# Blocks 4 and 5 of two weights loaded and converted one by one, three identity products fewer, and another order of the opening

## The chip, the core and the metric

The kernel runs on one core of a Trainium2 chip. Its engines run side by side, each through its own list of instructions in order: TensorE (PE in the profile, with its weight loads as PEld), VectorE (DVE), ScalarE (ACT), GpSimd (POOL), and SyncE (SP), which here only issues DMAs. They wait for each other through semaphores. The metric is device time in microseconds of one execution; lower is better. A time is the median of several runs.

## What is computed

Eight batches of eight heads, 576 tokens of 64 numbers each, first go through an attention over 32 memories, then all 4608 tokens through a bilinear feed-forward layer. Cut to what matters:

```python
def _attn_ref(q, k, v, phi):
    a = phi - np.max(phi, axis=2, keepdims=True)
    a = np.exp(a)
    a = a / (np.sum(a, axis=2, keepdims=True) + 1e-09)
    k_m = np.einsum('bhsm,bhsd->bhmd', a, k)
    v_m = np.einsum('bhsm,bhsd->bhmd', a, v)
    scores = scale * np.matmul(q, k_m.transpose(0, 1, 3, 2))
    scores = scores - np.max(scores, axis=-1, keepdims=True)
    attn = np.exp(scores)
    attn = attn / (np.sum(attn, axis=-1, keepdims=True) + 1e-09)
    return np.matmul(attn, v_m)

def _moe_ref(x, w1, w2, w3, w_out):       # 512 -> 1024 -> 1024 -> 512
    return ((x @ w1) * (x @ w2) @ w3) @ w_out
```

The four weights arrive as float64.

## The kernel before

**Weights first.** w3 and w_out have no function between them, so the kernel multiplies them once, in the opening: W = w3 w_out, by blocks of 128 rows k = 0 to 7 of the inner index. w3 is taken transposed and in two halves, w30 and w31; w30 gives the upper half of W (tokens X0 to X2 and W01 to W07 of the order, four PSUM banks), w31 the lower half (W10 to W17). `product` (lines 493 to 505) makes one such step: with all four row blocks it is four matmuls of 512 columns in float32, eight passes in the trace. X0, X1 and X2 are step 0 of w30 in pieces.

**Conversion.** No engine computes in float64, so each block is loaded as raw words (`raw`) and converted in five steps, C1 to C5 (`convert`, lines 422 to 489): sign (VectorE; ScalarE for the last ones), high and low (ScalarE, which read the raw words), shift and join (VectorE). The joined block is `w` (of w3) or `wo` (of w_out). A task is one such block, or a pair of blocks; w1 and w2 are converted in the same way, by quarters of columns. `groups` (lines 380 to 385) lists the tasks by the raw buffer that they share; there are five raw buffers of one megabyte. When the three steps that read the raw words of a group are recorded, the load of the group five further on is issued from SP (`fetch`). Loads use eight semaphores in turn.

**Attention and the gated product.** Of batch 0, in the opening: top, exp, norm (maxima, exponentials and sums of phi), bm and bs (maxima spread on TensorE and taken off on VectorE), be (the exponentials by token), mem (the memories), memc (kvm, on ScalarE), block and blockc, sc, mx, sb, ex, sm, mu, tr (scores and softmax), ah and al (the probabilities as two float32r parts). M0 to M3 join the memories with w1 and w2, of which Mh and Ml make two parts. The gated product (`ab_unit`, tokens A, a, g) is 12 matmuls of 288 columns on TensorE (A), a copy `a_sb` on ScalarE (a) and a product into `g` on VectorE (g). The output follows from g with the weights W in two parts, Wh and Wl. K copies the upper half of W out of PSUM; Kh and r cast parts of it to Wh on ScalarE.

**What sets the order.** All engines keep the order in which the program records them, and for the first batch that order is the table FIRST, a list of tokens such as C1 (the next task's sign step), W01 or -exp. SECOND and BATCH do the same for the later batches. Identity products at the very start (WARM of them, line 581) keep TensorE busy until the first real product.

Of the kernel before, what the change touches and what calls it, by code (L numbers as in the profile page):

```python
# [24 lines left out]
FIRST = """
C1 C1 C3 C2 C2 C4 C3 C4 C5 C1 C3 C5 C1 C2 C4 C2 C3 C4 C5 C5 C1 C2 C3 C4 C1 C5 C2 C3 C3 C1 C4 C5 C2 C2 C2 C4 C4 C1 C5
C1 C3 C2 C3 C5 C1 C3 C4 C4 C5 C1 C2 C3 C4 C5 C5 C2 C4 C1 C3 C5 phi0 kv0 C1 C1 C2 C3 C2 q0 X0 X1 X2 W01 C3 C4 C4 C5 C5
W02 W03 W04 W05 W06 C2 C1 C1 C4 C2 C4 W07 C3 C2 C3 -top C5 K1 -exp C5 -bm -bs W10 Kh1 K3 C4 -norm C1 K0 -be C3 -mem C5
Kl1 Kt0 r0 Kt3 Kt1 -memc Kh3 -block r3 C2 C3 K2 s0 Kt2 Kh0 r1 s1 -blockc C4 C1 C5 W11 -sc0 -sc1 -scc0 -scc1 -mx1 -mx0
-sb0 -sb1 C3 C2 C4 -ex0 C2 C3 C1 C5 C1 -sm0 C4 C2 C4 C5 C3 C2 -mu0 -tr0 C4 C1 -ex1 C5 -sm1 C1 C2 C3 C5 -mu1 -tr1 C1  # L30
-ah0 -al0 W12 W13 W14 W15 W16 M0 Mh0 M1 C3 -ah1 Mh1 C2 W17 C4 Ml0 Ml1 Dt0 C4 A a -al1 g phi A A C2 a C3 a Et0 Dt3 g C5
g s3 f0 C1 C5 A A t0 Kh2 Kl2 a a g Et3 C2 M2 Mh2 Dt2 Dt1 g Ml2 A a A C1 C4 g f1 F3 F2 F0 a top g C3 r2 q A a A C1 a C5
g g C3 C4 C5 kv F1 f2 z0 A A D2 a a Kl0 D3 w2 y2 M3 Mh3 g g E2 Et2 Ml3 w3 A A h0 a a Kl3 y3 f3 s2 E3 bm g g bs w1 y1
h2 A a A D0 t2 g l2 Et1 E0 S2 z2 be mem A exp norm D1 E1 memc a a l0 g g block O blockc w0 y0 h1 l1 h4 h3 t3 l4 t1 z1
z3 M0 sc0 scc0 mx0 sb0 O O l3 O O Mh0 h6 S3 S1 l6 h5 Ml0 l5 O S4 h7 p4 p1 h11 ex0 l7 O O h9 h8 C11 sm0 mu0 tr0 l8 sc1
q M1 l9 O u2 ah0 h10 l10 O h12 p5 Mh1 h13 scc1 l11 al0 l12 l13 O O O O C21 C22 Ml1 mx1 sb1 ex1 C12 sm1
"""
# [12 lines left out]


# [770 lines left out]
```

## Time and profile before

| | |
|---|---|
| median of 3 runs | 521.74 us (520.87 to 522.21) |
| span of the profiled execution | 519.8 us |
| TensorE busy | 511.9 us, 98% |
| VectorE busy | 383.8 us, 74% |
| ScalarE busy | 280.1 us, 54% |
| GpSimd busy | 145.0 us, 28% |
| DMA | 68.86 MB, 132 GB/s over the span |

The page gives one profiled execution; its own time is known by its span, from its first to its last instruction. A share of busy time is a mean over the whole span. The first 100 us hold the opening and the first batch, in which ScalarE and VectorE are much busier than later; for these the trace is read by stretches. In a row of the timeline the brackets give the idle time before an instruction and what ended it.

### The profile page before, as it was taken

To read this page: it belongs to the slowest core of one execution; us is meant where nothing else is said; L and a number is where in the kernel's file an instruction comes from. 1 tells how busy PE (TensorE), PEld (TensorE's weight loads), DVE (VectorE), ACT (ScalarE), POOL (GpSimd) and SP (SyncE) were. 2 spreads that over 40 slices of the span, in tenths; PEclk is the share of its full clock that TensorE was granted. 3 is DMA by queue.
4 is the path that set the end of the run, shared out by engine and by line. 5 is a ranking of instruction groups with operands and counts; after the bars stand their busy time and mean duration, and the time that the engine had idled before them with its cause. 6 is when DMAs were issued, how large, how long until landed. Compare 5 with 4: busy or idle time off the path is not lost.

```text
span 519.8 us, 11002 instructions
## 1 busy us (share of the span) xinstructions
PE 511.9 (98%) x4488; PEld 443.5 (85%) x4488; DVE 383.8 (74%) x655; ACT 280.1 (54%) x494; POOL 145.0 (28%) x158
## 2 busy tenths in 40 slices
...
GB/s 282 413 407 352 386 149 131 228 1 129 167 163 2 115 221 121 3 25 188 245 3 0 153 297 8 2 115 236 107 1 28 216 215 1 1 69 24 2 1 91
DMA packets 29794, 68.86 MB, mean 132 GB/s; under 512 B 1840, under 2 KB 10032, under 8 KB 29744
## 3 DMA queue, kind: packets, MB, share of 16 engines
...
q14 instruction: 15, 0.12, 0.1%
...
## 4 chain that ended last, share of the span: by engine, by line
PE 91%; DMA 6%; issue 1%; ACT 1%; DVE 1%; SPq 0%; DVEq 0%; ACTq 0%
PE ab L596 39%; PE o L658 15%; PE x L658 14%; PE ab L658 6%; PE ab L346 3%; PE x L498 3%; PE x L224 3%; PE o L498 2%; DMA raw<-in_w_out 2%; DMA ph<-in_phiT 2%; PE ab L274 2%; PE o L346 1%; PE x L346 1%; DMA raw<-in_w3T 1%; PE x L233 1%
## 5 line engine op out<-in xcount | busy, mean ns | idle before, releaser
L596 PE MATMUL ab<-ah,mh 128*128 128x288 f32 x512 | 154.5, 302 | 0.0
L596 PE MATMUL ab<-ah,ml 128*128 128x288 f32 x512 | 151.6, 296 | 0.0
L596 PE MATMUL ab<-al,mh 128*128 128x288 f32 x512 | 149.4, 292 | 0.0
L641 DVE TENSOR_TENSOR sl<-g,sh 128x576 fp32r<-128x576 f32 x112 | 92.9, 848 | 24.8 <-ACT sh L635 24.6
L596 PEld LDWEIGHTS ab<-ah,mh 128*128 128x128 f32 x512 | 96.2, 188 | 9.2 <-DVE ss L305 4.2
L608 DVE TENSOR_TENSOR g<-ab,a_sb 128x288 f32<-128x288 f32 x128 | 57.8, 452 | 58.2 <-PE ab L596 36.2
L605 ACT COPY a_sb<-ab 128x288 f32<-128x288 f32 x128 | 51.2, 401 | 90.4 <-PE ab L596 89.1
L635 ACT CAST sh<-g 128x576 fp32r<-128x576 f32 x112 | 74.6, 677 | 45.9 <-PE o L658 20.2
L596 PEld LDWEIGHTS ab<-al,mh 128*128 128x128 f32 x512 | 97.4, 190 | 0.2 <-issue 0.2
L596 PEld LDWEIGHTS ab<-ah,ml 128*128 128x128 f32 x512 | 96.0, 188 | 0.0
L614 POOL TENSOR_TENSOR g<-g,g 128x288 f32<-128x288 f32 x32 | 26.0, 838 | 221.5 <-DVE g L608 221.5
L658 PE MATMUL o<-sh,Wh 128*128 128x288 f32 x192 | 56.8, 296 | 0.0
L658 PE MATMUL o<-sh,Wl 128*128 128x288 f32 x192 | 56.6, 295 | 0.0
L658 PE MATMUL o<-sl,Wh 128*128 128x288 f32 x192 | 56.6, 295 | 0.0
L622 POOL TENSOR_TENSOR g<-g,g 128x288 f32<-128x288 f32 x32 | 28.4, 906 | 90.3 <-DVE sl L641 80.6
L658 PE MATMUL x<-sh,Wh 128*128 128x288 f32 x176 | 52.9, 300 | 0.0
L658 PE MATMUL x<-sh,Wl 128*128 128x288 f32 x176 | 51.9, 295 | 0.0
L658 PE MATMUL x<-sl,Wh 128*128 128x288 f32 x176 | 51.9, 295 | 0.0
L658 PEld LDWEIGHTS x<-sh,Wh 128*128 128x128 f32 x176 | 33.1, 188 | 7.4 <-PE ab L274 4.2
L658 PEld LDWEIGHTS o<-sh,Wh 128*128 128x128 f32 x192 | 36.1, 188 | 1.4 <-issue 0.9
L626 POOL TENSOR_TENSOR g<-g,g 128x288 f32<-128x288 f32 x32 | 36.2, 1159 | 0.0
L658 PEld LDWEIGHTS o<-sh,Wl 128*128 128x128 f32 x192 | 36.1, 188 | 0.0
...
## 6 DMA issues: line engine op xcount, KB each, us to landing
...
```

The lines of the kernel that those rows point to most:

```text
L224: nc.tensor.matmul(ps[t][h * M : (h + 1) * M, : 2 * D], lhsT=v["a"][:, (NT * i + t) * P + h * M : (NT * i + t) * P + (h + 1) * M], rhs=kvt ...
L346: nc.tensor.matmul(ps[t][g * M : (g + 1) * M], lhsT=vm[b % 2][d, g], rhs=w12_sb[q][d, :, g], start=True, stop=True,)
L498: nc.tensor.matmul(pw[r][i][:, cols], lhsT=x[:, i * P : (i + 1) * P], rhs=wos[k // half][:, k % half, cols], start=k == 0 and cols.start == 0,
L596: nc.tensor.matmul(banks[w][:, :HALF], lhsT=x[:, t, w, fc : fc + P], rhs=y[:, n, t * HALF : (t + 1) * HALF], start=i == 0, stop=i == len(t ...
L605: nc.scalar.copy(out=a_sb, in_=banks[0][:, :HALF])
L608: nc.vector.tensor_tensor(out=G[n, f // half][:, f % half], in0=banks[1][:, :HALF], in1=a_sb, op=ALU.mult)
L614: nc.gpsimd.tensor_tensor(out=low, in0=top, in1=low, op=ALU.subtract)
L622: gp(out=s2, in0=s2, in1=s3, op=ALU.subtract)
L626: gp(out=a12, in0=a12, in1=s2, op=ALU.subtract)
L635: nc.scalar.copy(out=hi, in_=src)
L641: nc.vector.tensor_tensor(out=lo, in0=src, in1=hi.bitcast(F32), op=ALU.subtract)
L658: nc.tensor.matmul(ps[j][:, :HALF], lhsT=piece(x, s, 2 * part + k)[:, jc], rhs=y[:, k], start=i in (1, 4, 2, 5) and part == 0 and k == 0 a ...
```

## The change

Blocks 4 and 5 of w30 and of w_out become single tasks, as blocks 0 to 3 are; before, each was a pair. Groups 4 and 5 then hold one block of both weights each, where they held the pair of w30 and the pair of w_out. The number of groups and of bytes stays. WARM goes from 18 to 15. FIRST is written in another order, with ten tokens more (two tasks more, of five steps each). SECOND and BATCH hold the same tokens as before, with other line breaks, and the lines behind FIRST have numbers higher by one.

```diff
-WARM = 18
+WARM = 15
 FIRST = """
-C1 C1 C3 C2 C2 C4 C3 C4 C5 C1 C3 C5 C1 C2 C4 C2 C3 C4 C5 C5 C1 C2 C3 C4 C1 C5 C2 C3 C3 C1 C4 C5 C2 C2 C2 C4 C4 C1 C5
...
+C1 C2 C2 C1 C3 C2 C4 C3 C2 C4 C5 C1 C5 X0 C3 C4 C3 C5 C1 C2 C4 C5 C1 C4 C3 X1 C2 C3 C5 C4 C1 C1 C2 C3 C5 C4 C2 C2 C1
...
-    groups += [[("w30", k, 1, slice(0, DF // 2)), ("wo", k, 1, slice(0, DF // 2))] for k in range(1, 4)]
-    groups += [[(kind, k, 2, slice(0, DF // 2))] for k in (4, 6) for kind in ("w30", "wo")]
+    groups += [[("w30", k, 1, slice(0, DF // 2)), ("wo", k, 1, slice(0, DF // 2))] for k in range(1, 6)]
+    groups += [[(kind, k, 2, slice(0, DF // 2))] for k in (6,) for kind in ("w30", "wo")]
```

Three places in the lists of the engines, a row for one instruction or a run of equal ones.

VectorE, the conversion of block 1 (L457 or L458 is a sign step, L482 or L483 a shift, L487 or L488 a join; `w_137` and `w_132` are blocks 0 and 1 of w30, `wo_84` is w_out's, `raw` of the second sign step without `w` is block 2's). Before:

```order
L457 TENSOR_SCALAR uw<-raw 128x512
L487 ISA w_137<-w_137,u 128x1024
L457 TENSOR_SCALAR u<-raw 128x512
L482 TENSOR_SCALAR wo_84<-wo_84 128x512
L487 ISA wo_84<-wo_84,uw 128x1024
```

And now:

```order
L488 ISA w_132<-w_132,u 128x1024
L483 TENSOR_SCALAR wo_84<-wo_84 128x512
L458 TENSOR_SCALAR uw<-raw 128x512
L458 TENSOR_SCALAR u<-raw 128x512
L488 ISA wo_84<-wo_84,uw 128x1024
```

The shift of w_out's block 1 moved ahead of the sign step of w30's block 2, its join stays behind it.

SP, the loads from block 3 on (`in_w3T` in the first rows is w30, later w31; `ph` and `a` are phi in its two layouts). Before:

```order
L419 DMA raw<-in_w3T 128x1024
L419 DMA raw<-in_w_out 128x1024
L419 DMA raw<-in_w3T 128x2x1024
L419 DMA raw<-in_w_out 128x2x1024
L419 DMA raw<-in_w3T 128x2x1024
L419 DMA raw<-in_w_out 128x2x1024
L419 DMA raw<-in_w3T 128x2x1024 x3
L144 DMA ph<-in_phiT 128x2x576
L146 DMA a<-in_phi_tok 128x1152
L154 DMA kv_223<-in_kv 128x2x1024
```

And now, from block 4 on:

```order
L420 DMA raw<-in_w3T 128x1024
L420 DMA raw<-in_w_out 128x1024
L420 DMA raw<-in_w3T 128x1024
L420 DMA raw<-in_w_out 128x1024
L420 DMA raw<-in_w3T 128x2x1024
L420 DMA raw<-in_w_out 128x2x1024
L420 DMA raw<-in_w3T 128x2x1024
L145 DMA ph<-in_phiT 128x2x576
L147 DMA a<-in_phi_tok 128x1152
L420 DMA raw<-in_w3T 128x2x1024
L155 DMA kv_225<-in_kv 128x2x1024
```

Block 4 of both weights comes ahead of block 5 of either; phi moved ahead of two pairs of w31, kv ahead of one. The last pair of w31 comes behind kv, ahead of q, in both.

ScalarE, the last instructions ahead of the conversion of w1's first quarter (`w_0_78`; L517 or L518 are the casts to Wh). Before:

```order
L517 CAST Wh_82<-raw_89 128x256
L517 CAST Wh_82<-raw_93 128x256
L472 ACTIVATE w_393<-raw 128x1024
L478 ACTIVATE uw<-raw 128x1024
L544 COPY raw_88<-ab 128x512
L517 CAST Wh_82<-raw_86 128x256
L517 CAST Wh_82<-raw_91 128x256
L478 ACTIVATE u<-raw 128x1024
L472 ACTIVATE w_0_78<-raw 128x1024
```

And now:

```order
L518 CAST Wh_82<-raw_89 128x256
L518 CAST Wh_82<-raw_91 128x256
L473 ACTIVATE w_390<-raw 128x1024
L246 ACTIVATE kvm<-ab,sm 128x128 x2
L479 ACTIVATE u<-raw 128x1024
L473 ACTIVATE w_400<-raw 128x1024
L518 CAST Wh_82<-raw_88 128x256
L479 ACTIVATE uw<-raw 128x1024
L545 COPY raw_86<-ab 128x512
L473 ACTIVATE w_0_78<-raw 128x1024
```

Two more such casts stood higher up in the list before, none does now: six came ahead of w1, now three, and the other three stand among the steps of the first batch's gated product.

## Rows read from the trace of the kernel before

**Rows 1.** The page, busy time, share of the span, instructions, by engine:

```profile
PE 511.9 (98%) x4488; PEld 443.5 (85%) x4488; DVE 383.8 (74%) x655; ACT 280.1 (54%) x494; POOL 145.0 (28%) x158
```

**Rows 2.** Stretches: length, then busy time of each engine, clock, DMA:

```profile
core 0: us, PE busy (x) PEld busy (x) DVE busy (x) ACT busy (x) POOL busy (x), PEclk, DMA share, GB/s
...
10.00:12.00 2.00, 1.92 (x5) 0.58 (x4) 1.18 (x4) 1.63 (x4) 0.00 (x0) 1.00 1.01 377
12.00:14.00 2.00, 0.43 (x1) 0.30 (x2) 1.86 (x5) 1.81 (x3) 0.00 (x0) 1.00 1.02 416
...
20.00:22.00 2.00, 1.88 (x5) 0.68 (x4) 1.94 (x3) 1.86 (x3) 0.00 (x0) 1.00 1.02 408
...
120.00:519.00 399.00, 396.45 (x3732) 366.90 (x3712) 284.99 (x486) 184.73 (x353) 107.80 (x114) 1.00 0.28 95
```

**Rows 3.** Timeline, TensorE's waits: start, length, engine, instruction, idle before:

```profile
13.56 6.71 PE L498 MATMUL ab<-wo,w 128*128 128x512 f32 x15 [1.65 <-DVE wo L487]
...
24.80 14.00 PE L498 MATMUL ab<-wo,w 128*128 128x512 f32 x32 [0.28 <-DVE wo L487]
...
41.26 1.95 PE L498 MATMUL x<-wo,w 128*128 128x512 f32 x4 [0.53 <-DVE a L212]
...
46.13 0.59 PE L254 MATMUL ab<-ident,kvm 128*128 128x128 f32 x2 [0.56 <-ACT kvm L245]
```

**Rows 4.** Stretches from 55 to 100 us, columns as in rows 2:

```profile
55.00:60.00 5.00, 5.00 (x13) 2.24 (x12) 4.90 (x9) 4.95 (x6) 0.00 (x0) 1.00 1.04 385
60.00:65.00 5.00, 5.00 (x13) 2.25 (x12) 4.96 (x7) 4.70 (x6) 0.00 (x0) 1.00 1.05 388
65.00:70.00 5.00, 5.00 (x33) 1.84 (x40) 4.12 (x8) 4.04 (x6) 0.00 (x0) 1.00 0.41 153
70.00:75.00 5.00, 5.00 (x30) 2.42 (x15) 4.14 (x9) 4.82 (x7) 0.00 (x0) 1.00 0.26 89
75.00:80.00 5.00, 5.00 (x40) 5.00 (x39) 4.29 (x8) 4.65 (x7) 0.23 (x1) 1.00 0.83 271
80.00:90.00 10.00, 10.00 (x85) 9.00 (x84) 9.16 (x15) 8.99 (x17) 7.27 (x8) 1.00 0.22 66
90.00:100.00 10.00, 10.00 (x84) 9.00 (x84) 8.76 (x16) 8.52 (x18) 7.61 (x9) 1.00 0.88 333
```

**Rows 5.** Line 596, the gated product, 73 to 104 us: min/median/max ns, first start:

```profile
L596 PE MATMUL ab<-ah,mh x62: 293/297/696, 73.8 to 103.6; 128*128 128x288 f32 x62
```

**Rows 6.** Identity products and first product (timeline); passes of four (chain of waits):

```profile
1.36 7.12 PE L582 MATMUL x<-ident 128*128 128x128 f32 x36 [1.36 <-POOL ident masks.py:199]
...
8.31 3.61 PE L498 MATMUL ab<-wo,w 128*128 128x256 f32 x12
...
58.56 1.72 PE o L498 x4
```

**Rows 7.** Timeline of VectorE around 12 us:

```profile
11.92 0.46 DVE L457 TENSOR_SCALAR u<-raw 128x512 uint16<-128x512 uint16 x1 [0.62 <-DMA raw<-in_w3T]
...
12.82 0.69 DVE L487 CUSTOM_DVE_ANT_0 wo<-wo,uw 128x1024 uint16<-128x1024 uint16 x1
```

**Rows 8.** Timeline of ScalarE, a high step of one block and of a pair:

```profile
14.42 0.69 ACT L472 ACTIVATE w<-raw 128x512 f32<-128x512 f32 x1 [0.61 <-DMA raw<-in_w3T]
...
18.26 1.18 ACT L472 ACTIVATE w<-raw 128x1024 f32<-128x1024 f32 x1 [0.59 <-DMA raw<-in_w3T]
```

**Rows 9.** Stretches from 6 to 10 us, columns as in rows 2:

```profile
6.00:8.00 2.00, 2.00 (x14) 2.00 (x14) 1.06 (x5) 1.13 (x4) 0.00 (x0) 1.00 0.92 304
8.00:10.00 2.00, 2.00 (x13) 1.82 (x12) 1.83 (x7) 1.55 (x4) 0.00 (x0) 1.00 1.02 393
```

**Rows 10.** ScalarE ahead of w1: stretch, timeline, and the casts (line 517):

```profile
50.00:55.00 5.00, 4.98 (x42) 2.44 (x42) 4.82 (x9) 2.69 (x4) 2.92 (x3) 1.00 1.05 385
...
52.81 1.36 ACT L478 ACTIVATE u<-raw 128x1024 uint16<-128x1024 uint32 x1 [2.31 <-DMA raw<-in_w]
...
L517 ACT CAST Wh<-raw x6: 378/406/412, 39.1 to 50.1; 128x256 fp32r<-128x256 f32 x6
```

More of the change, by code (lines that the diff above doesn't have):

```diff
@@ L23 @@
 ORDERED = {EngineType.SP, EngineType.PE, EngineType.Activation, EngineType.DVE, EngineType.Pool}
-WARM = 18
+WARM = 15
 FIRST = """
-C1 C1 C3 C2 C2 C4 C3 C4 C5 C1 C3 C5 C1 C2 C4 C2 C3 C4 C5 C5 C1 C2 C3 C4 C1 C5 C2 C3 C3 C1 C4 C5 C2 C2 C2 C4 C4 C1 C5
-C1 C3 C2 C3 C5 C1 C3 C4 C4 C5 C1 C2 C3 C4 C5 C5 C2 C4 C1 C3 C5 phi0 kv0 C1 C1 C2 C3 C2 q0 X0 X1 X2 W01 C3 C4 C4 C5 C5
-W02 W03 W04 W05 W06 C2 C1 C1 C4 C2 C4 W07 C3 C2 C3 -top C5 K1 -exp C5 -bm -bs W10 Kh1 K3 C4 -norm C1 K0 -be C3 -mem C5
-Kl1 Kt0 r0 Kt3 Kt1 -memc Kh3 -block r3 C2 C3 K2 s0 Kt2 Kh0 r1 s1 -blockc C4 C1 C5 W11 -sc0 -sc1 -scc0 -scc1 -mx1 -mx0
@@ L30 @@
[L30 to L34, printed above, removed]
@@ L35 @@
-z3 M0 sc0 scc0 mx0 sb0 O O l3 O O Mh0 h6 S3 S1 l6 h5 Ml0 l5 O S4 h7 p4 p1 h11 ex0 l7 O O h9 h8 C11 sm0 mu0 tr0 l8 sc1
-q M1 l9 O u2 ah0 h10 l10 O h12 p5 Mh1 h13 scc1 l11 al0 l12 l13 O O O O C21 C22 Ml1 mx1 sb1 ex1 C12 sm1
+C1 C2 C2 C1 C3 C2 C4 C3 C2 C4 C5 C1 C5 X0 C3 C4 C3 C5 C1 C2 C4 C5 C1 C4 C3 X1 C2 C3 C5 C4 C1 C1 C2 C3 C5 C4 C2 C2 C1
+C3 C5 C4 C4 C3 C1 C5 C2 C2 C1 C3 C4 C5 C3 C2 C5 phi0 C1 C3 C1 C4 kv0 C4 C5 X2 W01 C5 C2 W02 C1 C3 C3 C2 W03 C1 W04
+C4 C5 C2 C3 C4 C5 C1 C4 C5 C1 C2 q0 C4 C3 C2 C5 C4 C1 -top W05 C3 -exp W06 -norm C5 -bm C3 -bs -be W07 K1 K3 C2 W10
@@ new lines @@
+C1 Kt1 Kt3 C4 K2 -mem C1 Kh3 W11 r1 C2 -memc C5 C3 C4 C2 -block C1 C5 W12 -blockc -sc0 C4 Kh2 C3 C5 K0 -scc0 -mx0
+-sc1 Kt0 C1 C2 C3 W13 W16 -sb0 -scc1 C2 -ex0 -mx1 C3 C4 C2 C1 W15 C5 C1 -sm0 C3 C4 C4 C5 -sb1 C5 C2 -mu0 C3 C1 W14
+M0 C4 -ex1 -tr0 C5 -ah0 -sm1 M1 C1 -mu1 Mh0 Mh1 -al0 -tr1 C2 Ml0 r3 W17 C4 A Kt2 -ah1 Ml1 C1 A a g C3 -al1 C5 C2 A
+Dt1 a g C3 a Dt2 Dt3 g A C4 C2 A a C5 r0 a F2 g Dt0 C4 s0 s3 D2 g phi M2 Kl2 C2 Mh2 Ml2 A A a F1 s1 E2 g C1 C3 Et3 a
+top A r2 a C5 D3 g C4 A g Et2 C3 a Et0 F0 g q C1 A A C5 a f1 w1 g s2 a g t2 E3 M3 w2 f3 t0 Mh3 Kh0 A kv Kh1 Ml3 bm
@@ L37 @@
+bs y2 z0 a exp f2 h0 g F3 Et1 Kl3 be A A l0 a w3 z2 t3 D0 norm mem t1 y3 Kl1 h2 z1 a memc D1 g A h1 g A block E1 w0
+Kl0 l1 y1 a E0 a O h4 g blockc l2 g sc0 z3 M0 h3 O f0 O l3 l4 p1 h5 S2 scc0 S3 l5 mx0 y0 sb0 O h6 p4 S1 h7 ex0 O O
+l7 S4 l6 O h8 h11 O l8 sm0 l11 h9 Mh0 h10 l9 O C11 O Ml0 sc1 mu0 M1 l10 h12 u2 p5 Mh1 l12 tr0 h13 l13 ah0 scc1 mx1
+Ml1 q al0 O O sb1 O O C12 C22 ex1 C21 sm1
 """
 SECOND = """
-A A M2 M3 a a -mu1 -tr1 Mh2 -ah1 g -al1 g A A phi kv a Ml2 g A h0 Mh3 a a g Ml3 g top A A a g a g bm bs A A a a g g A
```

15 lines of the change are left out of this document (8 added, 7 removed).

## The prediction

> **What bounds the kernel now.** I read the page first: TensorE is busy in 98% of the span [rows 1], so only time in which it waits can be won. The table by stretches comes next. From 120 us on TensorE is busy 396.45 of 399 us [rows 2]: nothing is left to win there, and what has been won or lost when the first batch is over stays so to the end. The waits lie in the opening. The timeline names four: 1.65 us at 13.56, before the second k of the first weight product (W01), and 0.28 us at 24.80, before W04, both for VectorE's last conversion step of a w_out block; 0.53 us at 41.26 for VectorE's subtraction of the maxima; 0.56 us at 46.13 for ScalarE's kvm [rows 3]. With 0.12 us in the stretch 20 to 22 [rows 2] they make 3.1 us, the most that a better order of the opening can give.
>
> The same table tells who comes next. From 55 to 80 us, where the gated product's first matmuls come at 73.8, ScalarE is busy 23.16 of 25 us [rows 4, 5]; it is nearly as full as TensorE, and it must deliver every a_sb, ah and mh that TensorE needs.
>
> **Part 1, the identity products.** Eighteen products are 36 passes, and the first real product starts at 8.31 [rows 6]. Three fewer are six passes: at the mean of (8.31 - 1.36) / 36 = 0.19 us that is 1.2 us. By itself this gives nothing: W01, some 3.4 us of products later, waits 1.65 us anyway. TensorE's clock: the granted clock reads 1.00 in the stretches around that wait [rows 2]. The wait now left before W01 is at most 1.65 + 1.2 - 0.5 (part 2) = 2.4 us, longer than any that the rows show, so a fall of the clock to 1.2 GHz there is not excluded; I take nothing, and as a bound W01 at half pace, 3.4 us, which would use up the gain of the opening.
>
> **Part 2, W01.** Before, VectorE's sign step for block 2 stands ahead of the shift and the join of w_out's block 1. It starts at 11.92, after 0.62 us for its load; the join runs from 12.82 to 13.51; W01 starts at 13.56 [rows 3, 7]. Now shift and sign of w_out's block 1 stand ahead of that step, and only the join follows it: 11.92 plus some 0.4 us, then 0.69 us, then 0.05 us, 13.05. Gain 0.5 us.
>
> **Part 3, blocks 4 and 5 singly.** Work is added: on ScalarE the high step of a pair costs 1.18 us, of two singles 2 x 0.69 = 1.38 us [rows 8], 0.2 us more; its low step I take alike, so 0.4 us a pair and 0.8 us for the two pairs, and the same again on VectorE. Its cover is TensorE's backlog of W04 and W05, 2 x 3.44 us (1.72 us for four passes [rows 6], eight to a product); without it, W06 would start that much later. What it buys: the loads of w30 block 4 and wo block 4 now follow block 3 directly, so W04 no longer waits for both halves of two pairs. W01 at 13.05, three products of 3.44 us and some 0.15 us at W02, where the join becomes the later one: W04 at 23.5 against 24.80 [rows 3]. Gain so far 1.3 us, the 0.5 of part 2 included.
>
> The loads also go through SP's queue in smaller pieces. The rows show no loss: while half-megabyte loads land (8 to 14 us) the queues move 393, 377 and 416 GB/s, and with one-megabyte loads (20 to 22 us) 408 [rows 2, 9]. I take zero; the bound is the 304 GB/s of 6 to 8 us, while quarter-megabyte loads land [rows 9]. The Trainium skill's page "DMA: Bandwidth & Descriptors", section Bandwidth, speaks against this edit: it asks for a megabyte or more per DMA and measures 341 GB/s there. By its figure, called an estimate, the four half loads would take 0.9 us longer than at 408, and all behind them would land so much later. The trace disagrees: its half-size loads already move more than that figure.
>
> **Part 4, phi and kv moved ahead of w31 on SP.** phi and phi_tok go ahead of w31 blocks 2-3, kv ahead of blocks 4-5. Maxima, exp and kvm are then early, and W12 stands between the memories and the scores. I count the 0.53 and the 0.56 us as gone: 1.3 + 1.1 = 2.4 us. What is late next: w31 blocks 4-5 land after kv, so ScalarE and VectorE wait longer for them, by what phi and kv take to land; TensorE has W11 and W12 by then, and I cost it at nothing for TensorE. The gated product would so start about 2.4 us early, near 71.4. Bounds: 1.3 us if the two waits come back elsewhere, 3.1 us if all go.
>
> **Part 5, whether the first batch can keep it.** As many bytes stand ahead of w1's first quarter on SP as before, so it lands at the same time, and ScalarE, which waited 2.31 us for it until 52.81 [rows 10], starts on w1 and w2 no sooner. From there it must do all that it did, and more: before, six Wh casts of 0.41 us are over by then [rows 10]; now three, since ScalarE waits for w31 earlier on. That adds 3 x 0.41 = 1.2 us to the tight stretch. ScalarE's work from 52.81 to 100 us: 2.69 us of 50 to 55 less the 0.50 us up to its wait (52.81 - 2.31 = 50.50), 2.19; then 4.95 + 4.70 + 4.04 + 4.82 + 4.65 + 8.99 + 8.52 = 40.67 [rows 4, 10]; together 42.9 of 47.2 us, 91% busy. With the casts 44.1 us. It reaches the same point at 52.8 + 44.1 / s, s being its busy share:
> s = 0.95: 99.2, 0.8 us kept;
> s = 0.975: 98.0, 2.0 us kept;
> s = 0.934: 100.0, nothing kept;
> s = 0.91, as before: 101.3, 1.3 us lost.
> In the rows s is 0.965 from 55 to 65 and 0.95 from 70 to 80, where ScalarE is pushed; 0.88 from 80 to 100, where it waits for TensorE's products. If TensorE comes early, those last waits shrink, and VectorE (9.16 of 10 us from 80 to 90) makes new ones. I take 0.95, the row of 70 to 80, where conversions and a_sb copies already stand side by side. So 0.8 of 2.4 us is kept: ScalarE becomes the bound of the first batch, and most of the gain turns into small waits of TensorE between 73 and 100 us.
>
> **The sum.** The span of the profiled execution is 519.8 us; it would become 519.0. The median of the runs shown is 521.74, 1.9 us above it, for what the span leaves out; I carry that over unchanged: 520.9 us, 0.15% less. A measurement of this kernel can tell about 0.3%, 1.6 us, from no change.
>
> **Rivals.**
> Kept: ScalarE's waits before were only TensorE's pace, s rises to 0.97 or more, and 1.6 to 2.5 us stay. For it: 0.99 from 55 to 60. Against it: VectorE is as full, and a_sb goes PE, ACT, DVE, PE for each unit. Time 519.2 to 520.1.
> Lost: the moved casts and the new order of conversions hold up mh and al, s stays at 0.91 or falls, and the first batch ends 1.3 us or more late. It decides at s = 0.934. For it: s has been 0.91 over the whole stretch; the next batch's kv loads also wait for ScalarE's reads of the kv buffers, and the memories of batch 1 for these loads. Against it: part of that share was TensorE's pace. Time 523.0, and 523.4 at s = 0.90.
> Half loads slow: at 304 GB/s, four loads of 0.52 MB take 6.9 instead of 5.1 us; w1's first quarter lands 1.8 us later, ScalarE with it, and 0.8 won turns into 1.0 lost: 522.7. The rows of 8 to 14 us speak against it. By the figure of the Trainium skill's page "DMA: Bandwidth & Descriptors", section Bandwidth, the delay would be the 0.9 us of part 3, and the time about that of before.
> No effect: the opening wins nothing, because W01 and W04 wait for other steps, or because the clock falls before W01 (part 1); ScalarE then ends as before, 521.7. Against it: the order of VectorE's rows around W01, and a clock of 1.00 through 1.65 us of wait.
>
> **Chances.** Forecast (0.3 to 1.6 us faster) 0.48; kept 0.29; lost 0.17, of it 0.07 beyond 1.6 us; half loads slow 0.02; no effect 0.04. Faster by over 0.3%: 0.29. Slower by over 0.3%: 0.07. Within: 0.64. The range goes from 519.2 (2.5 us kept) to 523.0 (1.3 us lost): it leaves out about 0.05 below and 0.1 above.
>
> **What would show it.** Right: W01 near 13.0 and W04 near 23.5, without a wait of 0.28 us; no waits at the maxima and the kvm; the gated product's first matmul near 71.4; then TensorE waits of 0.1 to 0.8 us between 73 and 100 us that name ScalarE's or VectorE's instructions, some 1.6 us in all, with ScalarE at 0.95 from 55 to 80. Wrong: no such waits (kept); W01 still at 13.5 or W04 at 24.8 (parts 2, 3); the first wait for w1 ending well after 52.8 (half loads slow); a wait over 1 us at M1, M2 or at the memories of batch 1 (lost).

## The result: slower by 0.6%, and the profile after

The changed kernel takes 524.2 us (median of 6 runs) where the kernel before takes 521.47 (6 runs): the ratio is 1.0059, with a 95% interval of 1.0044 to 1.0074. The forecast was 520.9, its range 519.2 to 523.0. The profiled execution took 524.17 us, its span is 522.3 us, 2.5 more than before.

The page and the table by stretches of the changed kernel (length, busy time of PE, PEld, DVE, ACT and POOL, clock, DMA share, GB/s), to be set beside [rows 1, 2, 4]:

```profile
PE 512.0 (98%) x4482; PEld 442.1 (85%) x4482; DVE 385.3 (74%) x661; ACT 279.4 (53%) x498; POOL 144.2 (28%) x158
```

```profile
55.00:60.00 5.00, 5.00 (x13) 2.28 (x12) 4.90 (x10) 4.99 (x5) 0.00 (x0) 1.00 1.05 385
60.00:65.00 5.00, 5.00 (x16) 1.93 (x15) 5.00 (x7) 5.00 (x6) 0.00 (x0) 1.00 1.05 387
65.00:70.00 5.00, 3.89 (x37) 1.24 (x37) 4.90 (x9) 4.47 (x8) 0.00 (x0) 1.00 0.32 119
70.00:75.00 5.00, 5.00 (x30) 4.02 (x29) 4.73 (x9) 5.00 (x7) 0.00 (x0) 1.00 0.00 0
75.00:80.00 5.00, 5.00 (x45) 4.82 (x51) 4.83 (x10) 4.85 (x9) 1.71 (x2) 1.00 0.82 275
80.00:90.00 10.00, 9.34 (x74) 7.81 (x59) 9.00 (x17) 8.79 (x13) 7.21 (x9) 1.00 0.48 172
90.00:100.00 10.00, 9.21 (x94) 7.63 (x96) 8.11 (x17) 9.38 (x23) 5.87 (x8) 1.00 0.79 272
105.00:115.00 10.00, 10.00 (x95) 8.68 (x94) 7.67 (x15) 4.08 (x7) 7.83 (x10) 1.00 0.00 0
115.00:125.00 10.00, 8.11 (x61) 7.87 (x60) 9.93 (x13) 5.25 (x9) 6.61 (x6) 1.00 0.01 3
120.00:519.00 399.00, 398.97 (x3753) 369.12 (x3751) 288.60 (x494) 186.73 (x356) 106.92 (x114) 1.00 0.28 95
```

From 55 to 80 us ScalarE is busier than before (24.31 of 25 us against 23.16), VectorE is busy 14.80 of 15 us from 55 to 70 (13.98 before), and TensorE, full from 55 on in [rows 4], now stands still in four of these stretches. The worst, 1.89 of 10 us, is 115 to 125, where batch 0's output is formed and where VectorE is busy 9.93 us.

Marks on TensorE's timeline tell where time was won and lost; first the kernel before, then the changed one. The first gated product was at 73.80 before [rows 5, to a tenth]; the rows are M0 and M1 (L346, L347), the first gated product, the first output product of batch 0 and the first gated product of batch 1:

```profile
68.79 1.95 PE L346 MATMUL ab<-w,vm 64*32 64x512 f32 x32
...
104.98 0.38 PE L658 MATMUL o<-sh,Wh 128*128 128x288 f32 x1
...
130.69 0.29 PE L596 MATMUL ab<-ah,mh 128*128 128x288 f32 x1
```

```profile
64.97 1.09 PE L347 MATMUL ab<-w,vm 64*32 64x512 f32 x16
67.17 1.09 PE L347 MATMUL ab<-w,vm 64*32 64x512 f32 x16 [1.11 <-DVE w L488]
...
71.33 0.69 PE L597 MATMUL ab<-ah,mh 128*128 128x288 f32 x1
...
105.12 0.40 PE L659 MATMUL o<-sh,Wh 128*128 128x288 f32 x1
...
133.19 0.29 PE L597 MATMUL ab<-ah,mh 128*128 128x288 f32 x1
```

At M0 TensorE is 3.8 us ahead. M1 then waits 1.11 us for VectorE's last conversion step of a block of w1 or w2, and at the first gated product 2.47 us are left (71.33, forecast 71.4). By the first output product all of it is gone (+0.14). By batch 1 the kernel is 2.50 us late, and it stays so to the end (+2.5 in the span). So behind the opening the loss has two parts: 2.6 us given back under the gated product, and 2.4 us lost in batch 0's output stage, of which the prediction says nothing.

TensorE's waits from 0 to 135 us (total, count, longest) and their rows name the places, against [rows 3]:

```profile
PE o L659 <- DVE sl L642: 1.9, 1, 1.9
PE x L583 <- POOL ident masks.py:199: 1.4, 1, 1.4
PE ab L499 <- DVE wo L488: 1.1, 1, 1.1
PE ab L347 <- DVE w L488: 1.1, 1, 1.1
PE x L225 <- DMA kv<-in_kv: 0.8, 1, 0.8
PE ab L597 <- DVE ml L366: 0.6, 1, 0.6
```

```profile
12.34 11.96 PE L499 MATMUL ab<-wo,w 128*128 128x512 f32 x27 [1.14 <-DVE wo L488]
...
83.62 0.40 PE L597 MATMUL ab<-ah,mh 128*128 128x288 f32 x1 [0.63 <-DVE ml L366]
...
99.83 1.52 PE L225 MATMUL x<-kv,a 128*32 128x128 f32 x48 [0.79 <-DMA kv<-in_kv]
...
118.95 0.40 PE L659 MATMUL o<-sl,Wh 128*128 128x288 f32 x1 [1.89 <-DVE sl L642]
```

The waits at 24.80, 41.26 and 46.13 of [rows 3] are gone. In their place stand one at M1 (L347), one for the ml of M2, one for batch 1's keys and values, and one of 1.89 us for a low part `sl`.

What is behind that last one: an output unit of TensorE needs a high part `sh` (ScalarE, token h) and a low part `sl` (VectorE, `low_part`, token l) of one group of two g blocks; there are 14 groups. Groups 6 and 7 are read after GpSimd's sums S2 and S3, groups 8 and 9 after S1, 12 and 13 after S4. VectorE and GpSimd of the changed kernel:

```profile
112.95 1.34 DVE L642 TENSOR_TENSOR sl<-g,sh 128x576 fp32r<-128x576 f32 x1 [0.44 <-POOL Wl L522]
114.22 0.74 DVE L292 TENSOR_REDUCE st<-s_sb 128x18 f32<-128x576 f32 x1
114.99 1.35 DVE L296 TENSOR_TENSOR s_sb<-s_sb,st 128x576 f32<-128x576 f32 x1
116.27 3.90 DVE L642 TENSOR_TENSOR sl<-g,sh 128x576 fp32r<-128x576 f32 x3
120.10 0.74 DVE L304 TENSOR_REDUCE ss<-s_sb 128x18 f32<-128x576 f32 x1
120.87 0.77 DVE L305 TENSOR_SCALAR ss<-ss 128x18 f32<-128x18 f32 x1
```

```profile
111.10 1.82 POOL L522 TENSOR_TENSOR Wl<-sl,Wh 128x512 fp32r<-128x512 f32 x1
112.88 4.13 POOL L625 TENSOR_TENSOR g<-g,g 128x288 f32<-128x288 f32 x4
116.97 4.63 POOL L627 TENSOR_TENSOR g<-g,g 128x288 f32<-128x288 f32 x4
```

Group 5 waits 0.44 us for GpSimd, which still reads the buffer that it needs (token y0); then softmax steps of batch 1 and group 7 stand ahead of group 6, for which TensorE waits; and beside GpSimd one low part takes 1.3 us (3.90 / 3).

### The profile page after: what moved, and what is told of

Read it like the earlier page. It is cut to its first block, busy times and chain, and to the rows that moved or that the text cites. A ratio compares the mean times of both kernels' runs of the same rounds, so it can differ in the third digit from the quotient of the medians.

```text
span 522.3 us, 11009 instructions
## 1 busy us (share of the span) xinstructions
PE 512.0 (98%) x4482; PEld 442.1 (85%) x4482; DVE 385.3 (74%) x661; ACT 279.4 (53%) x498; POOL 144.2 (28%) x158
## 4 chain that ended last, share of the span: by engine, by line
PE 81%; DMA 9%; DVE 6%; issue 2%; SPq 1%; ACT 1%; DVEq 0%; ACTq 0%
PE ab L597 36%; PE o L659 15%; PE x L659 14%; DMA raw<-in_w3T 7%; PE ab L659 6%; PE ab L347 3%; PE x L225 2%; DMA kv<-in_kv 2%; DVE w L488 2%; PE ab L275 2%; PE o L347 1%; PE x L347 1%; DVE w L483 1%; SPq L420 1%; PE x L234 1%
## 5 line engine op out<-in xcount | busy, mean ns | idle before, releaser
L642 DVE TENSOR_TENSOR sl<-g,sh 128x576 fp32r<-128x576 f32 x112 | 95.5, 872 | 26.0 <-ACT sh L636 24.4
L615 POOL TENSOR_TENSOR g<-g,g 128x288 f32<-128x288 f32 x32 | 25.1, 810 | 196.2 <-DVE g L609 196.2
L623 POOL TENSOR_TENSOR g<-g,g 128x288 f32<-128x288 f32 x32 | 27.9, 891 | 89.6 <-DVE sl L642 80.9
L659 PEld LDWEIGHTS o<-sl,Wh 128*128 128x128 f32 x192 | 36.1, 188 | 2.1 <-DVE sl L642 2.1
```

The costliest lines, as they stand in the source:

```text
L615: nc.gpsimd.tensor_tensor(out=low, in0=top, in1=low, op=ALU.subtract)
L623: gp(out=s2, in0=s2, in1=s3, op=ALU.subtract)
L642: nc.vector.tensor_tensor(out=lo, in0=src, in1=hi.bitcast(F32), op=ALU.subtract)
L659: nc.tensor.matmul(ps[j][:, :HALF], lhsT=piece(x, s, 2 * part + k)[:, jc], rhs=y[:, k], start=i in (1, 4, 2, 5) and part == 0 and k == 0 a ...
```

## The experiments

A profile is one execution, and executions of one kernel mostly differ by up to 0.8 us either way from its median; so medians decide, and profiles tell where. Single marks are no better: e1_y0, e2_low, e3_both and e10_nosums run the changed kernel's lists up to the first output product, and their marks there lie between -1.18 and +0.14. In the table, marks are the kernel's profile less that of the kernel before (first gated product, first output product of batch 0, first gated product of batch 1); a ratio is to the kernel before on the same chip, with its 95% interval.

| kernel | median us | ratio | gated | output | batch 1 |
|---|---|---|---|---|---|
| changed kernel | 524.20 | 1.0059 (1.0044–1.0074) | -2.47 | +0.14 | +2.50 |
| e8_warm15 | 521.40 | 0.9996 (0.9987–1.0006) | -0.33 | -0.32 | -0.32 |
| e11_singles | 521.42 | 0.9999 (0.9990–1.0009) | -0.19 | -0.19 | -0.20 |
| e14_phikv | 532.14 | 1.0202 (1.0186–1.0218) | +10.02 | +10.02 | +10.02 |
| e1_y0 | 522.90 | 1.0028 (1.0017–1.0039) | -3.03 | -0.76 | +0.82 |
| e2_low | 522.92 | 1.0030 (1.0018–1.0042) | -3.14 | -0.38 | +1.53 |
| e3_both | 522.75 | 1.0023 (1.0014–1.0032) | -3.08 | -1.18 | +0.14 |
| e4_tail | 523.05 | 1.0033 (1.0021–1.0044) | -2.44 | -0.21 | +0.54 |
| e10_nosums | 521.79 | 1.0003 (0.9994–1.0012) | -2.07 | +0.14 | +0.31 |
| e5_read | 522.14 | 1.0012 (1.0003–1.0021) | -2.44 | -0.90 | +0.40 |
| e6_mem | 523.48 | 1.0043 (1.0028–1.0057) | -3.00 | -0.08 | +0.72 |
| e7_readmem | 522.81 | 1.0034 (1.0020–1.0047) | -2.54 | +0.09 | +0.89 |
| e9_kv | 522.31 | 1.0019 (1.0010–1.0027) | -3.34 | -1.55 | -0.25 |
| e12_kvg | 521.78 | 1.0008 (0.9999–1.0017) | -2.85 | -1.01 | -0.14 |
| e13_all | 522.41 | 1.0017 (1.0007–1.0027) | -1.43 | -0.75 | +1.04 |
| e15_nokv | 522.11 | 1.0010 (1.0000–1.0019) | -2.33 | -0.98 | +0.10 |
| e16_all_nosums | 520.24 | 0.9983 (0.9974–0.9991) | -1.68 | -0.97 | -0.63 |
| e17_before_nosums | 521.53 | 1.0003 (0.9994–1.0012) | +0.57 | +0.56 | +0.56 |
| e18_later | 521.67 | 1.0009 (1.0000–1.0018) | -2.70 | -2.00 | -0.36 |

### One part of the change alone, on the kernel before

**Fifteen identity products** (e8_warm15).

```diff
-WARM = 18
+WARM = 15
```

> The kernel before with 15 identity products instead of 18, and nothing else. Theory of the prediction: the first product of the weights comes 1.2 us earlier and the wait before its second k grows by as much, 1.65 to about 2.85 us; the clock stays at 1.00 through it; time as before, 521.4. Rival: the longer wait brings the granted clock to half, and the opening loses up to 3.4 us: 523 to 525.

521.40 us, no difference: part 1 of the prediction holds, and the clock rival is out for waits of this length. The first product comes 1.5 us earlier, and waits of 0.82 and 1.85 us before W01 take it back, at a granted clock of 1.00.

**Blocks 4 and 5 singly** (e11_singles); their steps follow each other, nothing else moves.

```diff
-    groups += [[("w30", k, 1, slice(0, DF // 2)), ("wo", k, 1, slice(0, DF // 2))] for k in range(1, 4)]
-    groups += [[(kind, k, 2, slice(0, DF // 2))] for k in (4, 6) for kind in ("w30", "wo")]
+    groups += [[("w30", k, 1, slice(0, DF // 2)), ("wo", k, 1, slice(0, DF // 2))] for k in range(1, 6)]
+    groups += [[(kind, k, 2, slice(0, DF // 2))] for k in (6,) for kind in ("w30", "wo")]
-C3 C4 C4 C5 C1 C2 C3 C4 C5 C5 C2 C4 C1 C3 C5 phi0 kv0
+C3 C4 C4 C5 C1 C2 C3 C4 C5 C5 C2 C4 C1 C3 C5 C1 C2 C3 C4 C5 C2 C4 C1 C3 C5 phi0 kv0
```

> The kernel before with blocks 4 and 5 of w3 and w_out loaded and converted singly and nothing else moved: steps of block 5 follow those of block 4. Theory of the prediction: W04 no longer waits 0.28 us at 24.80, since it needs block 4 alone; added steps on ScalarE and VectorE (0.8 us on each) lie beside TensorE's backlog; the 0.53 and 0.56 us at the maxima and the kvm take up what is won, since phi, keys and values land as before: 521.4. Theory work: the added 0.8 us reach the end, since ScalarE is full from 52 us: 522.2. Theory half loads: loads of half a megabyte are slower, and the time grows by 1 us or more: 522.4.

521.42 us: the added steps and the half-size loads cost nothing that can be measured. The theories of added work and of slow half loads fall.

**phi, keys and values ahead of w31** (e14_phikv).

```diff
-C1 C2 C3 C4 C5 C5 C2 C4 C1 C3 C5 phi0 kv0 C1
+C1 C2 phi0 C3 C4 C5 C5 C2 C4 C1 kv0 C3 C5 C1
```

> The kernel before with batch 0's phi, and its keys and values, loaded ahead of the second and third load of w31, as in the changed kernel, and nothing else. Theory of the prediction (its part 4): the waits of 0.53 us at the maxima and 0.56 us at the kvm vanish, the gated product starts some 1.1 us earlier; of that little reaches the end, since the later loads land when they did: 521.0 to 521.4. Theory loss: w31's later blocks land up to 9 us later, ScalarE's conversions of them with them, and TensorE waits at W12 or later for more than it won: 522 or more.

532.14 us, 10 us slower: the theory of loss, far above its least. TensorE's wait at the maxima, then two waits of ScalarE and the clock in a stretch of that wait:

```profile
49.76 1.19 PE L498 MATMUL x<-wo,w 128*128 128x512 f32 x1 [8.81 <-DVE a L212]
```

```profile
34.52 1.20 ACT L472 ACTIVATE w<-raw 128x1024 f32<-128x1024 f32 x1 [5.06 <-DMA raw<-in_w3T]
...
44.38 1.12 ACT L472 ACTIVATE w<-raw 128x1024 f32<-128x1024 f32 x1 [7.42 <-DMA raw<-in_w3T]
```

```profile
38.00:41.00 3.00, 2.76 (x8) 0.92 (x6) 0.92 (x1) 0.00 (x0) 0.00 (x0) 1.00 1.05 271
...
44.00:47.00 3.00, 0.00 (x0) 0.00 (x0) 0.23 (x1) 2.62 (x3) 0.00 (x0) 0.50 1.04 397
47.00:49.70 2.70, 0.00 (x0) 0.00 (x0) 2.65 (x5) 2.70 (x8) 0.65 (x1) 0.50 1.04 387
49.70:52.00 2.30, 2.24 (x3) 1.18 (x4) 2.27 (x4) 2.30 (x3) 2.05 (x4) 0.50 1.05 387
```

phi and the keys are there early, but the steps that use them still stand behind the conversions of w31 in ScalarE's and VectorE's lists, and those now wait for loads that come later. So the move alone loses; the changed kernel moves the engines' order with it. No run has that order without the move.

### The order of batch 0's output stage

**GpSimd's late step** (e1_y0), on the changed kernel.

```diff
-O f0 O l3 l4 p1 h5 S2 scc0 S3 l5 mx0 y0 sb0 O
+O f0 y0 O l3 l4 p1 h5 S2 scc0 S3 l5 mx0 sb0 O
```

> One GpSimd step of the changed kernel is moved: the low half of the third product's weights, block 0 (1.82 us at 111.10, behind the sums S2 and S3), goes ahead of S2, into 1.47 us in which GpSimd waits at 105.8. Nothing else moves. In the changed kernel TensorE waits 1.89 us at 118.95 in batch 0's output stage for a low part from VectorE. Theory GpSimd: this late step is the cause, since the low part of group 5 waits for the buffer that it reads, and the sums behind it come late; then the wait is gone, and the time falls from 524.2 to about 522.3 us. Theory VectorE order: only the 0.44 us that the low part of group 5 waited for it come back, 523.8 us, and a wait of about 1.4 us stays. Theory bound (ScalarE and VectorE are full over the whole first batch, so whatever one wait gives up returns in the next): 524.2.

522.90 us: 1.3 us come back, more than the 0.44 of one theory and less than the 1.9 of the other. The wait shrinks to 0.56 us, at 117.25.

**VectorE's order** (e2_low), on the changed kernel.

```diff
-l5 mx0 y0 sb0 O h6 p4 S1 h7 ex0 O O l7 S4 l6 O h8 h11 O l8 sm0
+l5 y0 O h6 p4 S1 h7 O O l6 S4 l7 mx0 sb0 O h8 h11 ex0 O l8 sm0
```

> Only the order of VectorE's steps in batch 0's output stage of the changed kernel is changed (with the exp of ScalarE that hangs on it): the low part of group 6, for which TensorE waits 1.89 us at 118.95, goes ahead of that of group 7, and the softmax maximum and subtraction of batch 1 (0.74 and 1.35 us at 114.22 and 114.99) go behind both. GpSimd's order stays. Theory VectorE order: the low part ends near 115.5 instead of 118.9, the wait is gone, and the time falls from 524.2 to about 522.3 us. Theory GpSimd (its late step and sums are the cause): the wait stays, 524.2. Theory bound: the wait goes to the next low parts or to the second scores, 523.7 to 524.2.

522.92 us: again 1.3, between what the order theory and the bound theory had forecast. The wait for group 6 is gone, and another, 1.18 us, stands at 122.74 for a later low part.

**Both** (e3_both: the two diffs together).

> Both edits in one on the changed kernel: the GpSimd step into its idle time ahead of S2, and VectorE's low part of group 6 ahead of group 7, maximum and subtraction behind. Theory VectorE order: as with that order alone, 522.3, at most 0.3 us less. Theory GpSimd: as with its step alone, 522.3. Theory bound: 523.7 or more.

522.75 us: the two gains do not add up. Both may be ways to the same thing, group 6's low part in time; no run shows that apart.

**The order before** (e4_tail): from the first output product on, the tokens stand as in the kernel before.

```diff
-O h4 g blockc l2 g sc0 z3 M0 h3 O f0 O l3 l4 p1 h5 S2 scc0 S3 l5 mx0 y0 sb0 O ...
+f0 l2 S2 g g O blockc y0 h4 h3 l4 z3 M0 sc0 scc0 mx0 sb0 O O l3 O O Mh0 h6 S3 S1 l6 ...
```

> The changed kernel up to the first output product of batch 0; from there on its steps stand in the order that they have in the kernel before. Whoever holds the output stage's order responsible (GpSimd's or VectorE's) expects the wait of 1.89 us at 118.95 gone and what TensorE is late at the end of the gated product, 0.35 us against the kernel before, kept: 521.5 + 0.35 = 521.9 us, at most 522.4. Theory bound (the first batch is full, whatever its order): 523.5 to 524.2. Theory work (the loss lies in what was added, the single blocks, and shows up anywhere): 524.2.

523.05 us, 1.15 less than the changed kernel. The wait is gone, yet 1.6 us are left against the kernel before, more than the 0.35 that I had expected: the order of the output stage alone does not bring the time back. Its profile is the fastest of its executions (+0.54 at batch 1), so no trace shows where the median one loses the rest.

**GpSimd's sums taken away** (e10_nosums), on the changed kernel; a part of the result is not formed.

```diff
-O h6 p4 S1 h7 ex0 O O l7 S4 l6 O
+O h6 p4 h7 ex0 O O l7 l6 O
```

> The changed kernel with the sums S1 and S4 of batch 0 left out (eight GpSimd steps, 8.8 us from 112.9 to 121.6), so that part of the result is not formed; all else in the same order. Theory contention: VectorE's low parts at 116.3 to 118.9 take 0.70 to 0.75 us instead of 1.3 once GpSimd is idle beside them; with the subtraction of the maximum some 2.5 us of VectorE's work fall away, and TensorE's wait of 1.89 us at 118.95 with them: 522.3 us. Theory order alone: a low part takes about 1.3 us in this place anyway, and the wait stays: 524.2.

521.79 us, 2.4 less, with the order of the changed kernel. VectorE's rows, to be set beside those of the changed kernel above:

```profile
112.92 0.76 DVE L642 TENSOR_TENSOR sl<-g,sh 128x576 fp32r<-128x576 f32 x1 [0.44 <-POOL Wl L522]
113.60 0.74 DVE L292 TENSOR_REDUCE st<-s_sb 128x18 f32<-128x576 f32 x1
114.38 0.76 DVE L296 TENSOR_TENSOR s_sb<-s_sb,st 128x576 f32<-128x576 f32 x1
115.06 2.15 DVE L642 TENSOR_TENSOR sl<-g,sh 128x576 fp32r<-128x576 f32 x3
117.13 0.75 DVE L304 TENSOR_REDUCE ss<-s_sb 128x18 f32<-128x576 f32 x1
117.91 0.17 DVE L305 TENSOR_SCALAR ss<-ss 128x18 f32<-128x18 f32 x1
```

Three low parts take 2.15 us instead of 3.90 (0.72 and 1.30 each), the subtraction 0.76 instead of 1.35, the small addition (L305) 0.17 instead of 0.77; the reductions take 0.74 to 0.75 either way. The Trainium skill's page "SBUF — State Buffer", section Who interferes with whom, says that a VectorE instruction with two SBUF inputs contends with a GpSimd instruction that reads SBUF, and that a reduction never does; the low parts, the subtraction and the reductions agree, and the small addition, which reads one input, is not covered by these two sentences. Order alone cannot be the cause, since the order is the same, nor can a wait for the sums' results, since no step up to group 6's low part (the second of the three), for which TensorE waits, reads what S1 or S4 writes; order decides how much of the contention TensorE feels.

### The gated product

**An earlier read** (e5_read), on e3_both. The kv buffer for w2's last part is free when ScalarE has read w1's third part; its last read goes ahead of another sign step.

```diff
-Ml1 C1 A a g C3 -al1
+Ml1 C3 A a g C1 -al1
```

> The kernel with both output-stage edits (e3_both, 522.75 us), with two steps of ScalarE's conversion exchanged: the low step of w1's third part, the last read that frees the kv buffer for w2's last part, goes ahead of the sign step of w2's third part (1.4 us) and one copy. Theory load: in the changed kernel w2's last part is issued at 74.53 (72.33 before, although TensorE is 2.47 us earlier), ScalarE waits 1.25 us for it at 81.21, and the waits that follow for VectorE's ml cost TensorE 0.7 to 1.45 us between 80 and 92 us. The issue then comes near 72.3, ScalarE's wait is gone, and the time falls by 0.7 to 1.4, to about 521.7. Theory bound (ScalarE is full from 52 to 100 us, and its share of busy time sets the end of the gated product): ScalarE has as much to do as before, 522.7.

522.14 us, 0.6 less (the intervals of the two ratios overlap). In the changed kernel that load is issued at 74.53, 2.2 us later than before (72.33), and ScalarE, the engine held to be the bound, waits for it; in e5_read it is issued at 73.04, and ScalarE does not wait. In e3_both, on which e5_read stands, it is issued at 73.93 and the wait is 0.34 us only, so that the 0.6 us are not shown to be this wait. ScalarE's timeline, the changed kernel, e3_both and then e5_read:

```profile
81.21 1.16 ACT L473 ACTIVATE w<-kv 128x1024 f32<-128x1024 f32 x1 [1.25 <-DMA kv<-in_w]
```

```profile
79.70 1.28 ACT L473 ACTIVATE w<-kv 128x1024 f32<-128x1024 f32 x1 [0.34 <-DMA kv<-in_w]
```

```profile
79.89 1.33 ACT L473 ACTIVATE w<-kv 128x1024 f32<-128x1024 f32 x1
```

**Memories later** (e6_mem on e3_both, e7_readmem on e5_read).

```diff
-norm mem t1 y3 Kl1 h2 z1 a memc D1 g A h1 g A block
+norm t1 y3 Kl1 h2 z1 a D1 g A mem h1 memc g A block
```

> The kernel with both output-stage edits (e3_both, 522.75 us), with batch 1's memories (and the scaling that reads them) put 12 matmuls of the gated product later on TensorE. In the changed kernel and in e3_both TensorE waits 0.8 to 0.9 us there for the load of batch 1's keys and values, which lands 9.3 us after its issue; in the kernel before 12 matmuls less stand behind the memories, and it waits for nothing. Theory load: the wait falls by up to 1.6 us of matmuls put ahead of it, time 521.9. Theory bound: the end of the gated product is set by ScalarE's or VectorE's last steps, and the wait returns at the next of them: 522.7.

> Both at once on e3_both: the early read of w1's third part and batch 1's memories 12 matmuls later. Theory load: the two gains add up, 0.7 to 1.4 and 0.8 us: 520.6 to 521.2, at or a little below the kernel before. Since the keys and values are issued when ScalarE has read the last part, an earlier chain brings them forward too, so that the sum may be smaller by the overlap: at most 521.9. Theory bound: 522.7.

523.48 and 522.81 us, 0.7 slower than without the edit in both, though the intervals overlap. The wait for the load is gone, and in e6_mem 1.42 us stand at 99.81 for ScalarE's a_sb copy, which lies behind four casts and a high part. The bound theory is right that the wait returns.

**Keys and values earlier** (e9_kv), on e5_read: the sign, low and join steps of w1's and w2's last parts change places, and batch 1's keys and values are loaded ahead of its queries.

```diff
-a C5 D3 g C4 A g Et2 C3 a Et0 F0 g q C1 ... Kh0 A kv Kh1
+a D3 g C4 C5 A g Et2 C3 a Et0 F0 g kv C1 ... Kh0 A q Kh1
```

> On the kernel with the early read (e5_read, 522.14 us): w2's last part is read (its low and sign steps) ahead of w1's last part, so that the first kv buffer is free some 3 us sooner, and batch 1's keys and values are loaded ahead of its queries instead of behind. Theory load: the keys and values are issued near 86 instead of 89.2 us, land near 95.5, and the wait of 0.65 to 0.9 us at batch 1's memories is gone, with nothing put in its place: 521.3 us. Theory bound (any wait taken out of the first batch returns as another, as it did when the memories themselves were put later): 522.1.

522.31 us, nothing won. The load is early and its wait gone; 0.84 us stand at 103.43 instead, where the first output product needs a bank that VectorE still reads for a low part of the weights. Bound theory again.

### The last waits, and a control

**A bank earlier** (e12_kvg), on e9_kv.

```diff
-O h4 g blockc l2 g sc0 z3 M0
+O h4 g g blockc l2 sc0 z3 M0
```

> As the kernel with the early keys and values, and VectorE's last gated step of batch 0 goes ahead of the copies of km and vm and of one low part. In e5_read the second half of batch 1's first memory weights stands 0.7 us still for the bank that this step frees. Theory order: 0.6 to 0.7 us less than without it, 520.6 if the keys and values bring what their theory says, below the kernel before. Theory bound: no change against the kernel without it.

521.78 us, 0.5 less (the intervals overlap), the stall inside M0 gone; the time of before, within the uncertainty.

**The two waits left** (e13_all on e12_kvg; e15_nokv is the same without e9_kv's edit).

```diff
-block E1 w0 Kl0 l1 y1 a E0 a O ... l8 sm0 l11 h9 Mh0 h10 l9 O
+block E0 E1 w0 Kl0 l1 y1 a a O ... l8 h9 l9 sm0 l11 Mh0 h10 O
```

> On the kernel with all edits so far (e12_kvg, 521.78 us), the two waits that its trace still shows in batch 0 are taken out by order: VectorE's last low part of the second product's weights goes ahead of a low part of the gated product (TensorE waits 0.86 us at 103.97 for the bank that it reads), and the low part of group 9 goes ahead of the softmax sum and of group 11 (TensorE waits 0.59 us at 121.07 for it). Theory order: both waits go, 1.2 to 1.45 us less, about 520.4 us, and the opening's 2.5 to 3 us are kept in good part. Theory bound (ScalarE's and VectorE's work over the whole first batch sets its end, whichever step TensorE happens to wait for): the waits show up at other steps, 521.8.

> As the kernel with all edits, but batch 1's keys and values and its queries loaded in the changed kernel's order, that is, with the keys and values last. Theory load: with the later waits gone, the 0.65 to 0.9 us for the keys and values count, and the time lies that much above the kernel with all edits: 521.2. Theory bound: no difference between the two.

522.41 and 522.11 us: the two waits are gone in both, and nothing is won; nor do the two differ by more than their intervals, as the bound theory had it. In e13_all the second scores and second memory weights wait instead, for steps that now come later on VectorE.

**The sums away from the best order, and from the kernel before** (e16_all_nosums, e17_before_nosums: S1 and S4 of FIRST left out, so that a part of the result is not formed).

> The kernel with all edits to the order (e13_all, 522.41 us) with the sums S1 and S4 of batch 0 left out, eight GpSimd steps, so that part of the result is not formed. Theory contention: in its output stage VectorE is full (the changed kernel: 9.93 of 10 us from 115 to 125) because GpSimd runs beside it and stretches its two-operand steps from 0.72 to 1.3 us; without these sums its waits go, the opening's gain is kept, and the time falls to about 520.3 us, below the kernel before. Theory ScalarE (the gain is used up before the output stage): 522 or little less.

> The control: the kernel before with the same sums S1 and S4 of batch 0 left out, so that part of the result is not formed. Its trace shows no wait of TensorE in the output stage, so both theories expect no change, 521.4 us. Were it faster, what the other run gains would lie in the work left out and not in the opening's gain.

520.24 us, 2.2 less than e13_all and 0.17% below the kernel before (0.9983, 0.9974 to 0.9991); the control stays at 521.53. The stretch 115 to 125 us, e13_all and then e16_all_nosums (TensorE's busy time is the second number, VectorE's the fourth):

```profile
115.00:125.00 10.00, 9.58 (x88) 7.74 (x86) 9.88 (x15) 4.98 (x9) 6.28 (x6) 1.00 0.09 30
```

```profile
115.00:125.00 10.00, 10.00 (x96) 8.77 (x95) 8.64 (x16) 6.05 (x11) 0.00 (x0) 1.00 0.18 46
```

So with the sums left out of both, the kernel with all edits is 1.3 us faster than the kernel before: part of the opening's gain lasts, and it is lost where VectorE is slowed by GpSimd. In the changed kernel's own order (e10_nosums) only the time of before comes back; there the gain is used up ahead of the output stage.

**Softmax behind the sums** (e18_later), on e13_all, with nothing left out.

```diff
-l6 S4 l7 mx0 sb0 O h8 h11 ex0 O l8 h9 l9 sm0 l11 Mh0 h10 O C11 O Ml0 sc1 mu0 M1 l10 h12 u2 p5
+l6 S4 l7 O h8 h11 O l8 h9 l9 mx0 Mh0 h10 O C11 O Ml0 sc1 l10 sb0 M1 ex0 l11 sm0 h12 u2 mu0 p5
```

> The kernel with all edits to the order (e13_all, 522.41 us), nothing left out; only batch 1's softmax steps on VectorE and ScalarE (subtraction, exp, sum, scaling) stand later, behind the stretch in which GpSimd runs, and the low parts, the result C11 and the ml of batch 1 that free TensorE's banks stand ahead of them. In e13_all TensorE spends 1.5 us more than the kernel before on the second scores, the second memory weights and the products around them (118.98 to 125.22), waiting for just these steps. Theory contention: this 1.5 us goes, 520.9 us, below the kernel before, as when the sums were left out. Theory late softmax: ah of batch 1 is ready only near 130 us, and the first gated product of batch 1 waits: 522 or more.

521.67 us, 0.7 less, but not the 520.9 expected. The 1.5 us are gone; the edit made a new wait. TensorE's timeline, and ScalarE's:

```profile
123.88 0.40 PE L660 MATMUL o<-sh,Wh 128*128 128x288 f32 x1 [1.30 <-ACT c L677]
```

```profile
122.05 0.68 ACT L300 ACTIVATE s_sb<-s_sb 128x576 f32<-128x576 f32 x1 [3.56 <-DVE s_sb L296]
```

I had put the exp on ScalarE ahead of the copy that frees TensorE's bank, and the exp waits 3.56 us for VectorE. With the exp behind that copy this wait should go; that was not tried. No complete kernel here is faster than the kernel before.

## Why the prediction was wrong, point by point

- **Bound of the opening and the gain (the number right, by luck).** The waits at 24.80, 41.26 and 46.13 are gone, the gated product starts at 71.33 (forecast 71.4). But two errors cancel. TensorE reaches M0 3.8 us early, more than the 3.1 us that I called the most: that bound counts waits alone, and the identity products left out let the first product start 1.15 us earlier as well (7.16 against 8.31). Then M1 waits 1.11 us for VectorE, ahead of the stretch for which I forecast waits.
- **Part 1 (right).** Fifteen identity products change nothing (521.40); the clock stays at 1.00 through the wait of 1.14 us.
- **Part 2 and the places of W01 and W04 (a size off, to the good).** W01 starts at 12.34 instead of the forecast 13.05, W04 at 22.85 instead of 23.5. I had kept VectorE's sign step for block 2 at 11.92, behind a wait for its load; it starts at 11.26, without a wait. In part this is the execution: in five other kernels with the same opening W01 starts at 12.38 to 12.82.
- **Part 3 (right).** Singles cost nothing that can be measured (521.42). The Trainium skill's page "DMA: Bandwidth & Descriptors", section Bandwidth, asks for 1 MiB or more per DMA; by its 341 GB/s, measured with DMAs issued from GpSimd, my estimate was some 0.9 us more (2.10 MB at 341 instead of 408 GB/s is 1.0 us when redone). The run shows no such loss.
- **Part 4 (right in the sum, wrong as a step by itself).** The two waits vanish. But the move alone costs 10 us (e14_phikv): it needs the order of ScalarE's and VectorE's steps that goes with it, which I counted at nothing.
- **Part 5 (right in size up to 95 us, its reason only in part).** I forecast 0.8 of 2.4 us kept at 100 us. The 145th gated matmul starts at 94.85 against 95.69, 0.84 kept. ScalarE's share was 0.97 from 55 to 80 us (forecast 0.95) and 0.94 from 55 to 100. But ScalarE also waited, 1.25 us for a load whose issue hangs on its own order of reads. Then the wait for batch 1's keys and values (0.79 us, 1.0 with what follows it), which I had named under "Lost", takes the rest: +0.14 at the first output product, 0.9 us worse than forecast.
- **The step that failed is the sum.** It ends with the gated product, since [rows 2] show TensorE full from 120 us on, and I took what is won or lost there as final. Behind it, from 105 us to batch 1, lies the output stage, whose tokens the diff also rewrites; no term stands for it. The trace ends 2.5 us late where 0.8 early was forecast: of these 3.3 us the output stage holds 2.4 (+0.14 to +2.50), the 0.9 above are the rest. What the runs showed in its place is VectorE, slowed beside GpSimd's sums just where TensorE needs a low part: without the sums 2.4 us come back at the same order (e10_nosums), and the kernel before, without them, gains nothing (e17_before_nosums). The trace of before already had the warning, in rows that I did not read: VectorE's low parts take longer there beside GpSimd too, 2.23 us for two:

```profile
113.30 2.23 DVE L641 TENSOR_TENSOR sl<-g,sh 128x576 fp32r<-128x576 f32 x2
```

- **The rivals.** "Lost" had the right sign and one right mechanism, the loads of keys and values, and one of its signs came, a wait over 1 us at M1. But 1.3 us at 100 us was its size (its 523.4 at s = 0.90 is 523.5 when redone), and its reasons end there too. "Kept" asked for 0.97 or more of ScalarE; from 55 to 80 us that came, and nothing was kept. "Half loads slow" and "no effect" are out.
- **What stays open.** Orders alone brought the complete kernel to 521.67 and 521.78, 0.3 above the kernel before on the same chip, and whether a better one goes below it is not known. The split into 0.9 and 2.4 us is that of one execution. With the order of before in the output stage (e4_tail) 1.6 us of the loss stay, and no trace tells where the median execution loses them. Why e13_all is slower than e12_kvg by 0.6 is only partly told by the traces, and their intervals overlap.
